# A gated recurrence feeding a feed-forward block: tanh of the input gate written in place, more load buffers, and a new order of the whole program

## The chip, the core and the metric

The kernel runs on one core of a Trainium2 chip. A core has five engines that run their own instruction streams and meet only at semaphores: TensorE (PE in the profile, with its weight loads apart as PEld), VectorE (DVE), ScalarE (ACT), GpSimd (POOL) and SyncE (SP), which here issues all transfers but one. Each engine executes in order: an instruction that waits holds up all behind it. The metric is the time of one execution on the device, in microseconds. The kernel before took 522.07 us, the median of six runs (520.51 to 523.22).

## The reference

Inputs are x, r_gate and i_gate of shape (4, 5824, 256) in float32, a_param (256), and four weight matrices. What is computed, cut to what matters:

```python
sig_r, sig_i = 1 / (1 + exp(-r_gate)), 1 / (1 + exp(-i_gate))
a_t = exp(8.0 * sig_r * log(a_base))          # a_base: sigmoid of a_param, clipped
x_gated = sqrt(max(1 - a_t * a_t, 1e-6)) * sig_i * x
for t in range(S):
    h = a_t[:, t] * h + x_gated[:, t]         # h = 0 at the start of each of 4 sequences
    y[:, t] = h
a = y @ w1; b = y @ w2                        # 256 -> 1024
out = ((a * b) @ w3) @ w_out                  # 1024 -> 1024 -> 256
```

## The kernel before

The 23296 tokens are cut into 47 chunks: two of 256 tokens, 44 of 512, one of 256. A chunk c goes through a chain of steps, each of which is one small function with a one-letter name. The letters are those of the order quoted below; a number after them is the chunk, and further numbers are the half (the 256 channels are two blocks of 128) or the part.

- r, i, x (line 128): SP loads the three inputs, 512 KB each, tokens on the partitions, into the pool `loads`, which has three buffers for each of the three names.
- R and I (lines 137, 139, 146): ACT takes tanh of half of r and of i (a sigmoid is a tanh, scaled and shifted). Tanh of i goes to a tile of its own, th_i, in float32, with two buffers.
- p, t (lines 151, 167, 170): one is added to th_i in place, and it is multiplied by x, which gives u in bfloat16.
- V, U (lines 177, 188): th_r and u are turned, so that channels lie on the partitions: for the chunks in TURN_R and TURN_U by PE with the identity, into PSUM, for all others by a DMA transpose that SP issues, into SBUF.
- d, s, q, g (lines 199 to 224): ACT makes the decay a = exp(...); its square comes from ACT, DVE or POOL; ACT takes the root; DVE multiplies root and u.
- h, y (lines 241 to 250): DVE runs the recurrence as a scan, one for each half; the result is cast to bfloat16.
- a, b (line 260): PE makes eight blocks of 128 columns of y @ w1 (a) and y @ w2 (b). A block of a takes one PSUM buffer, b two blocks at a time.
- c, m (lines 274, 276, 288): ACT or DVE copies a to SBUF, DVE multiplies it with b out of PSUM.
- D, e, o (lines 299, 274 or 276, 318): PE multiplies with the folded matrix w3 @ w_out, ACT or DVE copies the result out, SP stores it.

The fold of w3 and w_out into one matrix is computed at the start in eight pieces: Lw3 loads, Cw3 casts, Ft transposes on PE, Fc copies out, Fm multiplies, Fe copies out with a scale (lines 345 to 407). The first D needs all eight. W steps are groups of eight matmuls of the identity with itself (line 255), with a result that nobody reads. PSUM has two pools: `psum_o` with four buffers, which a, D, the turned tiles and the fold share, and `psum_b` with two, which b and W share. A buffer is taken in the program's order, and is free when the reader of its former tile is done.

Nothing of the order is found at run time. All steps stand in one long text, ORDER, and the program issues them word by word in that order; each engine so gets its own part of the text. The sets ahead of it tell which engine does a step: DV_ names a step given to DVE, AC_, FOLD_ACT and W_ACT to ACT, and POOL has what is left where it can. The order begins so:

```
i1 r1 E A3. A0. A1. A2. r0 I1 R1 i0 R0 V1 V0 W1 W12 I0 x1 d1.0 s1.0 t1.1 W2 x0 U1 d0.0 W0 d0.1 t0.1 d1.1 s0.0
s1.1 Lw1.0 Lw2.0 Cw1.0 r2 Lw1.1 s0.1 q1 g1 U0 i2 q0 Cw2.0 Lw2.1 R2 W15 W4 r3 W3 W8 Lw3.2 g0 h0.0 W7 W6 h0.1
```

Of the kernel before, what the change touches and what calls it, by code (L numbers as in the profile page):

```python
# [10 lines left out]
F32 = mybir.dt.float32  # L11
BF16 = mybir.dt.bfloat16
AF = mybir.ActivationFunctionType
# [9 lines left out]
def kernel(  # L23
# [12 lines left out]
    nc = tc.nc  # L36
    P = 128
    B, S, D = x.shape
# [17 lines left out]
    loads = ctx.enter_context(tc.tile_pool(name="loads", bufs=3))  # L56
    gates = ctx.enter_context(tc.tile_pool(name="gates", bufs=2))
# [20 lines left out]
    T = {}  # L78

    TURN_R = {0, 1, 2, 3, 4, 7, 12}  # L80
    TURN_U = {0, 1, 2, 3, 4, 6, 7}
    DV_TIMES = {0, 1}
    DV_PLUS = set()
    DV_HALF = {(8, 0)}
    DV_SQUARE = {(0, 0), (1, 1)}
    AC_SQUARE = {(3, 1), (4, 1), (5, 0), (5, 1), (7, 0), (8, 1), (9, 0), (11, 0), (11, 1), (12, 0), (12, 1), (13, 0),
        (13, 1), (14, 0), (14, 1), (15, 1)}
    DV_CAST = {1, 2}
    AC_CAST = {0}
# [35 lines left out]
    def load(c, nm):  # L125
        n = sizes[c] // P
        t = loads.tile([P, 4, D], F32, name=nm + "_t", tag=nm)
        nc.sync.dma_start(  # L128
            out=t[:, :n, :],
            in_=src[nm][starts[c]:starts[c] + sizes[c], :].rearrange("(p n) c -> p n c" if long_rows(c) else "(n p) c -> p n c", p=P))  # L130
        T[nm, c] = t
# [11 lines left out]
    def tanh_i(c):  # L143
        n = sizes[c] // P
        t = gates.tile([P, 4, D], F32, name="th_i", tag="th_i")
        nc.scalar.activation(out=t[:, :n, :], in_=T["i", c][:, :n, :], func=AF.Tanh, scale=0.5)  # L146
        T["thi", c] = t
# [261 lines left out]
    def last(c):  # L409
# [21 lines left out]
        i1 r1 E A3. A0. A1. A2. r0 I1 R1 i0 R0 V1 V0 W1 W12 I0 x1 d1.0 s1.0 t1.1 W2 x0 U1 d0.0 W0 d0.1 t0.1 d1.1 s0.0  # L431
        s1.1 Lw1.0 Lw2.0 Cw1.0 r2 Lw1.1 s0.1 q1 g1 U0 i2 q0 Cw2.0 Lw2.1 R2 W15 W4 r3 W3 W8 Lw3.2 g0 h0.0 W7 W6 h0.1
        h1.0 h1.1 x2 V2 W10 y0 a0.0.1 a0.0.0 b0.0 d2.0 y1 d2.1 I2 W9 a0.1.0 c0.0.0 c0.0.1 m0.0 a1.0.1 a1.0.0 a0.1.1
        b0.1 c0.1.0 c0.1.1 m0.1 a1.1.0 s2.0 Cw1.1 c1.0.0 c1.0.1 Cw2.1 Lwo.1 a0.2.0 c0.2.0 R3 b1.0 a1.1.1 m1.0 W13
        a0.3.0 c0.3.0 b1.1 c1.1.0 a0.3.1 a0.2.1 s2.1 c1.1.1 m1.1 Lwo.0 b0.2 p2 Cw3.2 b0.3 Lw3.0 c0.2.1 a1.2.0 Ft2 m0.2
        c0.3.1 m0.3 b1.2 a1.2.1 q2 c1.2.0 Fc2 c1.2.1 m1.2 t2.0 t2.1 Cwo.1 Cwo.0 r4 W11 V3 U2 Lw3.1 a1.3.0 W14 Lw3.4
        d3.0 d3.1 W5 Fm2 Cw3.0 c1.3.0 g2 h2.0 h2.1 i3 i4 a1.3.1 b1.3 Ft0 R4 Fe2 V4 c1.3.1 Lw3.7 y2 Cw3.4 Fc0 a2.0.0
        a2.0.1 b2.0 Cw3.1 d4.0 d4.1 a2.2.0 m1.3 c2.0.0 I3 s3.0 s4.0 s3.1 c2.2.0 c2.0.1 m2.0 Ft4 a2.1.0 s4.1 I4 a2.1.1
        b2.1 Fm0 Fc4 x3 q3 Lw3.5 Fm4 c2.1.0 c2.1.1 m2.1 Ft1 Lw3.6 p3 Fe0 Fe4 Fc1 Cw3.7 Ft7 a2.3.0 a2.2.1 b2.3 t3.0
        Lw3.3 Fc7 r5 a2.3.1 c2.2.1 t3.1 Cw3.5 U3 c2.3.0 r7 c2.3.1 q4 p4 g3 Cw3.6 Fm1 Ft5 Cw3.3 Ft6 b2.2 Fe1 Fc5 h3.0  # L440
        h3.1 y3 Fm7 R5 Fm5 Fe5 x4 Ft3 Fc6 i5 Fm6 Fc3 t4.0 Fe7 r6 a3.1.0 R7 Fe6 a3.1.1 V5 Fm3 m2.2 c3.1.0 c3.1.1 a3.0.0
        V7 I5 d7.0 c3.0.0 m2.3 i6 r9 t4.1 x5 U4 d7.1 Fe3 g4 h4.0 h4.1 R6 r8 V6 x6 r11 a3.0.1 b3.0 p5 y4 I6 d5.0 t5.0
        b3.1 D0.0 D0.1 e0.0 c3.0.1 m3.0 m3.1 R9 D1.0 D1.1 a3.2.0 e1.0 s5.0 d5.1 s7.0 a3.3.0 a3.2.1 b3.2 b3.3 c3.2.0
        t5.1 o0.0 i7 U5 c3.3.0 c3.2.1 d6.0 a4.0.0 a3.3.1 x7 d6.1 p6 s7.1 s5.1 s6.0 s6.1 m3.2 t6.0 a4.1.0 a4.0.1 b4.0
        o1.0 c4.0.0 t6.1 c3.3.1 m3.3 r10 c4.1.0 R8 a4.3.0 D2.0 D2.1 V8 a4.2.0 c4.0.1 c4.3.0 q5 m4.0 c4.2.0 a4.1.1 e2.0
        g5 i8 h5.0 h5.1 q6 q7 c4.1.1 D2.2 a4.3.1 a4.2.1 D2.3 b4.1 D3.0 D3.1 b4.2 e2.1 y5 m4.1 I7 c4.3.1 V9 e3.0 d8.0
        a5.0.0 d8.1 i10 c4.2.1 m4.2 o2.1 x8 o2.0 b4.3 a5.0.1 I8 p7 R10 c5.0.0 c5.0.1 s8.0 t7.0 i9 t7.1 U6 b5.0 a5.2.0
        a5.1.0 m4.3 d9.0 s8.1 g6 o3.0 m5.0 c5.1.0 D4.0 D4.1 s9.0 c5.2.0 R11 b5.1 a5.1.1 p8 e4.0 c5.1.1 h6.0 D3.2 d9.1
        t8.0 h6.1 m5.1 t8.1 D3.3 a5.3.0 U7 g7 e3.1 r12 V10 o4.0 y6 c5.3.0 I9 I10 h7.0 a5.2.1 b5.2 a5.3.1 a6.1.0 c5.3.1
        d10.0 d10.1 c5.2.1 b5.3 D4.2 m5.2 m5.3 D4.3 c6.1.0 h7.1 R12 e4.1 p10 a6.0.0 a6.0.1 s9.1 b6.0 x10 c6.0.0 a6.2.0  # L450
        c6.0.1 r13 a6.2.1 a6.1.1 o3.1 m6.0 c6.2.0 c6.1.1 q9 a6.3.0 b6.1 c6.2.1 b6.2 m6.1 q8 s10.0 a6.3.1 V12 x9 U8 i11
        D5.0 b6.3 m6.2 c6.3.0 c6.3.1 m6.3 V11 p9 t10.0 t10.1 r14 D5.1 U10 y7 s10.1 t9.0 d12.0 a7.1.0 R13 i13 a7.0.0
        d12.1 e5.0 V13 c7.1.0 a7.0.1 x11 r15 b7.0 a7.2.0 b7.1 a7.2.1 t9.1 g8 d11.0 c7.0.0 c7.0.1 h8.0 h8.1 o4.1 I11
        D6.0 a7.1.1 m7.0 d11.1 c7.2.0 c7.1.1 m7.1 I13 D6.1 y8 s11.0 a7.3.0 c7.2.1 c7.3.0 b7.2 a7.3.1 c7.3.1 e6.0 d13.0
        d13.1 a8.0.0 a8.1.1 a8.1.0 D5.2 b7.3 m7.2 D5.3 U9 c8.0.0 x13 R14 c8.1.0 c8.1.1 m7.3 r16 a8.0.1 g9 p11 h9.0
        s11.1 q10 h9.1 c8.0.1 e5.1 q11 D6.2 D6.3 t11.0 t11.1 p13 t13.0 y9 o6.0 o5.0 U11 V14 R15 b8.0 g10 m8.0 e6.1
        D7.0 a8.2.0 D7.1 b8.1 e7.0 c8.2.0 m8.1 a8.3.0 h10.0 a8.3.1 s13.0 s13.1 a9.0.0 t13.1 c8.3.0 d14.0 h10.1 c8.3.1
        a8.2.1 c9.0.0 c8.2.1 b8.2 a9.0.1 b8.3 a9.1.0 i12 x12 i15 r17 o5.1 y10 m8.2 a9.1.1 m8.3 c9.0.1 c9.1.0 D7.2 I12
        D7.3 c9.1.1 b9.0 b9.1 a9.2.0 V15 I15 a9.3.0 d14.1 R16 i16 r19 o6.1 p12 t12.0 t12.1 m9.0 s14.0 e7.1 c9.2.0
        a10.0.0 a9.3.1 c9.3.0 m9.1 d15.0 p15 c10.0.0 g11 h11.0 h11.1 V16 o7.0 D8.0 c9.3.1 s12.0 s14.1 s15.0 D8.1 x15  # L460
        a9.2.1 U13 R19 i14 a10.0.1 U12 e8.0 d16.0 I16 d16.1 b9.2 D8.2 a10.2.0 b9.3 D8.3 c9.2.1 m9.2 m9.3 c10.0.1 y11
        d15.1 a10.2.1 a10.3.0 b10.0 e8.1 c10.2.0 c10.2.1 s15.1 c10.3.0 a10.1.1 a10.1.0 b10.1 a10.3.1 m10.0 R17 s16.0
        a11.0.0 s12.1 t15.0 t15.1 p16 I14 s16.1 b10.2 c10.1.0 c10.1.1 m10.1 m10.2 p14 a11.2.0 b10.3 c10.3.1 a11.0.1
        a11.1.0 r18 o8.0 x14 x16 b11.0 m10.3 t14.0 q12 t14.1 c11.0.0 o7.1 b11.1 g12 h12.0 h12.1 c11.1.0 U15 D10.0 q13
        c11.2.0 q14 D10.1 c11.0.1 y12 V17 D10.2 D10.3 a11.1.1 t16.0 e10.0 e10.1 c11.1.1 a11.2.1 c11.2.1 x18 q15 q16
        m11.0 m11.1 g13 h13.0 o8.1 V19 i18 a11.3.0 a11.3.1 o10.0 c11.3.0 c11.3.1 D9.0 h13.1 y13 b11.2 D9.1 a12.0.0
# [103 lines left out]
    for word in ORDER.split():  # L570
        name, args = re.fullmatch(r"([LC]w[123o]\.|A\d\.|[A-Za-z]+)([\d.]*)", word).groups()
# [29 lines left out]
```

## Time and profile before

| | before |
|---|---|
| median of six runs | 522.07 us (520.51 to 523.22) |
| the profiled execution | 520.51 us |
| its span, first to last instruction | 518.7 us |
| granted TensorE clock | 1.0 |
| DMA queue of SP: bytes, share of 16 engines | 123.5 MB, 85.4% |
| DMA transposes: number, median from issue to landing | 80, 4.7 us (of r) and 4.2 us (of u) |
| loads of 512 KB: median from issue to landing | 5.5 us (r), 5.5 us (i), 5.1 us (x) |
| table loads on ACT | 34, 1.28 us each |

The span is what the profile covers; what lies around it is 1.8 us. Busy times of PE are not PE at its peak: a matmul is in the pipeline longer than it keeps the next from starting, so the time from one start to the next tells more. "Idle before, releaser" in a row is how long the engine stood before that instruction and what ended it.

### The profile page before, as it was taken

The numbers are of one execution on the slowest core, as the hardware profiler recorded it, in microseconds if no ns is written. First come the engines' busy times: TensorE is split into PE (matmuls) and PEld (weight loads), VectorE is DVE, ScalarE is ACT, GpSimd is POOL, SyncE is SP. The second block draws the span as 40 slices with busy tenths as digits, with TensorE's granted clock in tenths as the row PEclk, the third lists the DMA queues.
The fourth block names the chain that finished last, engine by engine and source line by source line (L and its number), as shares of the span: only waits on it lengthen the run. The fifth ranks groups of instructions, "written<-read, shape, count | busy, mean of one in ns | idle before, by whom it ended". The sixth has DMA issues, their size and how long they took to land.

```text
span 518.7 us, 9092 instructions
## 1 busy us (share of the span) xinstructions
PE 499.7 (96%) x3259; PEld 313.7 (60%) x3313; DVE 437.7 (84%) x422; ACT 466.1 (90%) x715; POOL 314.2 (61%) x268
## 2 busy tenths in 40 slices
PE   5879999999999999999999999999999999999997
PEld 5757665556565566556556565565665566566656
DVE  5998999999999798699898779798788976959853
ACT  6988999999999999999999999999999859968443
POOL 2674856665746855966789956868662767361300
PEclk9999999999999999999999999999999999999999
DMA  8995999999999999979699988999799468452212
GB/s 297 411 412 182 278 346 305 255 311 287 309 264 264 259 273 268 260 206 274 181 309 266 266 236 214 254 317 260 202 246 282 131 209 160 108 180 63 61 62 102
DMA packets 178338, 124.09 MB, mean 239 GB/s; under 512 B 87410, under 2 KB 173940, under 8 KB 178292
## 3 DMA queue, kind: packets, MB, share of 16 engines
q1 hardware_dynamic: 178288, 123.50, 85.4%
q8 instruction: 26, 0.43, 0.4%
q14 instruction: 20, 0.16, 0.1%
q10 hardware_dynamic: 4, 0.00, 0.0%
HBM read 78.91 MB, written 23.86 MB: 198 GB/s over the span
## 4 chain that ended last, share of the span: by engine, by line
PE 77%; DVE 15%; issue 4%; ACT 2%; DMA 1%; SPq 0%; DVEq 0%; ACTq 0%
PE po L299 25%; PE pb L260 25%; PE pa L260 24%; DVE g_t L288 5%; DVE h_t L241 4%; DVE sa L274 3%; DVE nrm L224 1%; PE pw L370 1%; DMA x_t<-in_x_dram 1%; DVE nrm L221 1%; PE ptw L359 1%; ACT sa L276 0%; PE ptr L177 0%; SPq L128 0%; DVE u_t L167 0%
## 5 line engine op out<-in xcount | busy, mean ns | idle before, releaser
L288 DVE TENSOR_TENSOR g_t<-sa,pb 128x1024 bf16<-128x1024 bf16 (+1 forms) x188 | 218.6, 1179 | 64.6 <-PE pb L260 35.6
L260 PEld LDWEIGHTS <-w_sb 128*128 128x128 bf16 x1504 | 146.5, 98 | 150.4 <-issue 8.1
L276 ACT CAST sa<-pa 128x512 bf16<-128x512 f32 (+1 forms) x331 | 179.5, 591 | 28.1 <-PE pa L260 20.9
L260 PE MATMUL pa<-y_t,w_sb 128*128 128x512 bf16 (+1 forms) x720 | 187.7, 372 | 4.6 <-DVE w3t L274 2.9
L260 PE MATMUL pb<-y_t,w_sb 128*128 128x512 bf16 (+1 forms) x730 | 182.7, 372 | 3.0 <-DVE g_t L288 1.1
L299 PE MATMUL po<-wp_sb,g_t 128*128 128x256 bf16 x1456 | 176.8, 273 | 0.5 <-DVE g_t L288 0.4
L299 PEld LDWEIGHTS <-g_t 128*128 128x128 bf16 x1456 | 142.3, 98 | 39.7 <-DVE g_t L288 0.7
L250 POOL CAST y_t<-h_t 128x1024 bf16<-128x1024 f32 (+1 forms) x44 | 51.5, 1170 | 144.9 <-DVE h_t L241 132.9
L241 DVE TENSOR_TENSOR_SCAN h_t<-a_t,h_t,nrm 128x512 f32<-128x512 f32 (+1 forms) x92 | 126.4, 1399 | 2.0
L170 POOL TENSOR_TENSOR u_t<-th_i,x_t 128x512 bf16<-128x512 f32 (+1 forms) x89 | 118.0, 1340 | 2.2 <-DMA x_t<-in_x_dram 1.1
L209 POOL TENSOR_TENSOR nrm<-a_t 128x512 f32<-128x512 f32 (+1 forms) x76 | 88.4, 1176 | 13.5 <-ACT a_t L199 13.5
L276 ACT COPY ot<-po 128x512 f32<-128x512 f32 (+1 forms) x87 | 51.1, 590 | 15.7 <-PE po L299 14.2
L199 ACT ACTIVATE a_t<-rt,la 128x512 f32<-128x512 bf16 (+1 forms) x80 | 64.7, 824 | 0.2
L151 POOL TENSOR_SCALAR th_i<-th_i 128x1024 f32<-128x1024 f32 (+1 forms) x45 | 52.2, 1160 | 20.4 <-ACT th_i L146 20.2
L224 DVE SCALAR_TENSOR_TENSOR nrm<-nrm,ut 128x1024 f32<-128x1024 f32 (+1 forms) x40 | 54.0, 1353 | 0.1
L146 ACT ACTIVATE th_i<-i_t 128x1024 f32<-128x1024 f32 (+1 forms) x47 | 49.0, 1047 | 0.5 <-DMA i_t<-in_i_gate_dram 0.4
L213 ACT ACTIVATE nrm<-nrm 128x1024 f32<-128x1024 f32 (+1 forms) x47 | 48.3, 1039 | 0.2
L139 ACT ACTIVATE th_r<-r_t 128x1024 bf16<-128x1024 f32 (+1 forms) x40 | 42.3, 1060 | 0.3 <-DMA r_t<-in_r_gate_dram 0.3
L274 DVE CAST sa<-pa 128x512 bf16<-128x512 f32 (+1 forms) x45 | 26.5, 617 | 1.1 <-PE pa L260 0.4
L213 ACT ACT_TABLE_LOAD x17 | 21.8, 1283 | 1.4 <-DVE nrm L209 1.1
L199 ACT ACT_TABLE_LOAD x9 | 11.5, 1283 | 0.2
L255 PE MATMUL warm<-ident 128*128 128x128 bf16 x128 | 9.9, 238 | 0.3 <-DVE g_t L288 0.3
(58 smaller groups left out, 128.7 us busy)
## 6 DMA issues: line engine op xcount, KB each, us to landing
out_dram<-ot SPq DMA_DIRECT2D x90, 256.0 KB, 3.9
r_t<-in_r_gate_dram SPq DMA_DIRECT2D x44, 512.0 KB, 5.5
i_t<-in_i_gate_dram SPq DMA_DIRECT2D x44, 512.0 KB, 5.5
x_t<-in_x_dram SPq DMA_DIRECT2D x44, 512.0 KB, 5.1
wf<-in_moe_w_dram SPq DMA_DIRECT2D x12, 512.0 KB, 9.6
wf<-in_moe_w_out_dram SPq DMA_DIRECT2D x2, 512.0 KB, 11.1
i_t<-in_i_gate_dram SPq DMA_DIRECT2D x3, 256.0 KB, 4.5
r_t<-in_r_gate_dram SPq DMA_DIRECT2D x3, 256.0 KB, 3.3
```

Source lines behind the costliest of these rows:

```text
L151: (nc.vector if c in DV_PLUS else nc.gpsimd).tensor_scalar(t, t, 1.0, 1.0, op0=ALU.add, op1=ALU.mult)
L170: (nc.vector if (c, half) in DV_HALF else nc.gpsimd).tensor_mul(out=u, in0=t, in1=xt)
L199: nc.scalar.activation(out=a, in_=pr, func=AF.Exp, scale=la4[:, cb:cb + 1], bias=la4[:, cb:cb + 1])
L209: (nc.vector if (c, cb) in DV_SQUARE else nc.gpsimd).tensor_mul(out=n, in0=a, in1=a)
L213: nc.scalar.activation(out=T["n", c][:, :, :w], in_=T["n", c][:, :, :w], func=AF.Sqrt, scale=-1.0, bias=1.0)
L224: nc.vector.scalar_tensor_tensor(out=T["n", c][:, :, :w], in0=T["n", c][:, :, :w], scalar=1e-3, in1=T["pu", c][:, :, :w], op0=ALU.max, op1 ...
L241: nc.vector.tensor_tensor_scan(h[:, cb, :], a[:, cb, :], n[:, cb, :], init, ALU.mult, ALU.add)
L250: eng.tensor_copy(out=T["y", c][:, :, :w], in_=T["h", c][:, :, :w])
L260: nc.tensor.matmul(out=dst[:, :w], lhsT=w_sb[:, cb, m * P:(m + 1) * P], rhs=T["y", c][:, cb, :w], start=(cb == 0), stop=(cb == NCB - 1))
L276: nc.scalar.copy(out=dst, in_=src_ps)
L288: nc.vector.tensor_mul(out=T["g", c][:, 2 * mp:2 * mp + 2, :w], in0=T["sa", c, mp][:, :, :w], in1=T["pb", c, mp][:, :, :w])
L299: nc.tensor.matmul(out=po, lhsT=T["g", c][:, k, j * P:(j + 1) * P], rhs=wp_sb[:, k, :], start=(k == 0), stop=(k == KD - 1), skip_group_che ...
```

## The change

Three things are changed. First, tanh of the input gate is written over the tile that was loaded, so there is no tile th_i any more, and p and t work on the load's tile. Second, the loads get buffers of their own numbers: four for r, five for i, four for x, in place of three each. Third, the order and the sets that tell which engine does a step are replaced as a whole. Chunk 5's u is turned by PE instead of by a DMA. The counts: DVE has 37 copies of a instead of 45, no cast of y instead of two, six evacuations instead of four; ACT has 339 copies of a instead of 331, two casts of weights instead of five, 86 evacuations instead of 88; POOL has 46 casts of y instead of 44 and eleven of weights instead of eight. ACT loads its tables 34 times in both. The order's text differs in nearly every line.

```diff
-    TURN_U = {0, 1, 2, 3, 4, 6, 7}
+    TURN_U = {0, 1, 2, 3, 4, 5, 6, 7}
...
-    DV_HALF = {(8, 0)}
-    DV_SQUARE = {(0, 0), (1, 1)}
+    DV_HALF = {(2, 0)}
+    DV_SQUARE = {(0, 0), (1, 0), (10, 0)}
...
-    DV_CAST = {1, 2}
-    AC_CAST = {0}
+    DV_CAST = set()
+    AC_CAST = {4}
...
-    DV_EVAC = {(2, 1), (5, 0), (9, 0), (9, 1)}
-    FOLD_ACT = {('c', 3), ('c', 6), ('e', 1), ('e', 2), ('e', 6)}
-    W_ACT = {('w2', 1), ('w3', 0), ('w3', 1), ('w3', 2), ('w3', 5)}
-    W_DVE = {('w1', 0)}
+    DV_EVAC = {(1, 0), (2, 0), (3, 1), (5, 1), (9, 0), (9, 1)}
+    FOLD_ACT = {('c', 7), ('e', 0), ('e', 1), ('e', 2), ('e', 3), ('e', 7)}
+    W_ACT = {('w2', 0), ('w3', 6)}
+    W_DVE = {('w1', 1)}
+    LOAD_BUFS = {"r": 4, "i": 5, "x": 4}
...
-        t = loads.tile([P, 4, D], F32, name=nm + "_t", tag=nm)
+        t = loads.tile([P, 4, D], F32, name=nm + "_t", tag=nm, bufs=LOAD_BUFS[nm])
...
-        t = gates.tile([P, 4, D], F32, name="th_i", tag="th_i")
-        nc.scalar.activation(out=t[:, :n, :], in_=T["i", c][:, :n, :], func=AF.Tanh, scale=0.5)
+        t = T["i", c]
+        nc.scalar.activation(out=t[:, :n, :], in_=t[:, :n, :], func=AF.Tanh, scale=0.5)
```

The beginning of the new order, as far as the first matmul of chunk 4 (a4.0.1):

```
r0 r1 E A3. A0. A1. i1 R1 R0 W3 V1 I1 V0 W13 W12 A2. W9 d1.0 d1.1 s1.0 i0 W15 I0 x0 t0.1 W14 d0.0 s0.0 s1.1
d0.1 s0.1 q0 x1 t1.1 Lw1.0 r3 Lw2.0 r2 q1 R3 Lw1.1 i2 W11 U0 g0 h0.0 Lw2.1 Cw1.0 W10 W2 U1 W0 W7 R2 W4 h0.1
Lw3.2 x2 g1 y0 W8 Lwo.0 Cw2.0 a0.1.0 a0.1.1 h1.0 c0.1.0 h1.1 a0.0.0 a0.0.1 V2 c0.1.1 d2.0 c0.0.0 W6 y1 b0.0
c0.0.1 d2.1 I2 Cw1.1 a1.0.1 a1.0.0 b0.1 a1.1.0 a0.2.0 c1.0.0 c1.0.1 Cw2.1 p2 a0.2.1 Cw3.2 m0.0 m0.1 c1.1.0
Lwo.1 b1.0 m1.0 t2.0 r4 W1 c0.2.0 a1.1.1 a0.3.0 t2.1 Cwo.0 W5 c1.1.1 Ft2 c0.2.1 a1.3.0 s2.0 b1.1 c0.3.0 b0.2
U2 a1.3.1 s2.1 Cwo.1 i3 Fc2 V3 x3 Lw3.0 q2 Lw3.1 i4 Lw3.4 m1.1 c1.3.0 Fm2 R4 g2 h2.0 h2.1 d3.0 Lw3.7 c1.3.1
m0.2 d3.1 Lw3.5 Fe2 a1.2.0 a0.3.1 b1.2 a1.2.1 I3 c0.3.1 V4 s3.0 d4.0 d4.1 b0.3 y2 c1.2.0 Cw3.0 c1.2.1 m1.2
a2.0.0 a2.1.0 b1.3 m0.3 a2.2.0 b2.0 m1.3 a2.2.1 c2.0.0 Lw3.3 a2.0.1 s4.0 c2.2.0 s3.1 p3 t3.0 c2.1.0 Cw3.1 Ft0
c2.0.1 c2.2.1 Fc0 m2.0 Cw3.4 b2.1 I4 s4.1 q4 r7 t3.1 a2.3.0 a2.1.1 Fm0 b2.2 p4 Cw3.5 c2.1.1 Ft4 c2.3.0 m2.1
Fe0 Ft1 a2.3.1 U3 Lw3.6 q3 Fc4 c2.3.1 Fc1 Fm4 Cw3.7 b2.3 Ft5 g3 Fe4 Fc5 Ft7 x4 Cw3.3 R7 r5 h3.0 h3.1 Fm1 Fm5
Fc7 Fe5 Ft3 Fm7 Fe1 Cw3.6 V7 Fe7 y3 Ft6 Fc3 d7.0 d7.1 Fc6 m2.2 Fm3 i6 r6 a3.1.0 Fe3 R5 Fm6 a3.1.1 c3.1.0
c3.1.1 t4.0 Fe6 t4.1 i7 i5 x5 U4 a3.0.0 R6 D0.0 a3.0.1 D0.1 I6 c3.0.0 e0.0 m2.3 g4 a3.3.0 a3.2.0 b3.0 h4.0
h4.1 b3.1 c3.0.1 m3.0 D1.0 a3.3.1 D1.1 I5 c3.3.0 y4 V5 r8 m3.1 a3.2.1 V6 b3.2 I7 e1.0 c3.2.0 c3.2.1 c3.3.1
b3.3 m3.2 m3.3 p5 a4.0.1
```

## The prediction

> **What bounds the kernel now.** First the busy shares, then what one matmul costs in the chain of waits (columns: start, length, what), then the engines in stretches of 20 us.
>
> ```profile
> PE 499.7 (96%) x3259; PEld 313.7 (60%) x3313; DVE 437.7 (84%) x422; ACT 466.1 (90%) x715; POOL 314.2 (61%) x268
> ...
> 173.57 1.73 PE pb L260 x8
> 175.73 1.75 PE po L299 x16
> ```
>
> Eight up-projection matmuls of 512 columns start within 1.73 us, 0.216 us each; sixteen of 256 columns within 1.75, 0.109 each. From the program: 44 full chunks x 32 x 0.216 = 304.1; three half chunks x 32 x 0.109 = 10.5; 1456 down-projections x 0.109 = 159; the fold's 64 matmuls 7.0 and 64 transposes 3.6 (0.0555 each); 96 turning transposes 5.3. Together 490 us of PE work that no order removes (128 warm-up matmuls, 7 us, are filler). The span is 518.7: everything to be won is 28.7 us. A rule of the Trainium skill ("Perfetto Trace Analysis", Identifying the Most-Contended Engine) judges PE's headroom by the share of weight loading: 60% here, 205 us free. The matmuls' own starts leave 28.7; I use these.
>
> ```profile
> core 0: us, PE busy (x) PEld busy (x) DVE busy (x) ACT busy (x) POOL busy (x), PEclk, DMA share, GB/s
> 0.00:20.00 20.00, 12.69 (x154) 11.86 (x155) 13.26 (x36) 15.19 (x23) 6.55 (x13) 1.00 0.90 336
> 20.00:40.00 20.00, 16.20 (x173) 12.79 (x172) 19.26 (x30) 18.32 (x24) 16.66 (x15) 1.00 1.04 412
> 40.00:60.00 20.00, 19.84 (x163) 13.98 (x164) 17.77 (x23) 18.66 (x27) 9.97 (x10) 1.00 0.75 197
> 60.00:80.00 20.00, 19.73 (x132) 12.58 (x133) 19.55 (x22) 19.93 (x29) 13.04 (x12) 1.00 1.10 345
> 80.00:100.00 20.00, 19.74 (x123) 11.43 (x124) 19.58 (x21) 19.71 (x29) 13.55 (x11) 1.00 1.04 256
> 100.00:120.00 20.00, 18.95 (x116) 11.25 (x116) 19.76 (x21) 19.67 (x30) 10.44 (x9) 1.00 1.09 306
> ...
> 480.00:500.00 20.00, 19.89 (x124) 12.17 (x125) 15.82 (x15) 10.65 (x20) 4.39 (x6) 1.00 0.21 65
> 500.00:520.00 20.00, 15.67 (x128) 12.33 (x126) 6.75 (x8) 6.68 (x16) 0.24 (x1) 0.98 0.23 79
> ```
>
> 19.89 of 20 is a saturated PE. The loss lies in the first 33 us, in small gaps from 60 to 140 us, and in the last evacuation and store (the last matmul starts at 515.5, 3.2 us to the end). In 60 to 120 DVE and ACT both have 19.6 of 20: two engines limit PE there at once. The first saturated moment is in the order of time, PE alone:
>
> ```profile
> 29.41 0.62 PE L177 MATMUL ptr<-ident,th_r 128*128 128x128 bf16 x8 [0.21 <-ACT th_r L137]
> 32.88 1.02 PE L260 MATMUL pa<-y_t,w_sb 128*128 128x512 bf16 x3 [2.85 <-DVE w3t L274]
> ```
>
> By 32.88 PE has done chunks 0 and 1 (64 x 0.109 = 7.0), 48 turning transposes (2.7) and 1.8 of the fold: 11.4. So 21.5 us are lost before it; 28.7 - 21.5 - 3.2 leaves 4.0 for gaps after it. Those are the three pots.
>
> **The change part by part.**
>
> Buffers and Tanh in place. Tanh keeps its instruction and size (1.076 us, 128x1024); only its target moves. A load tile of the input gate is now held until the product, five buffers for the three plus two of before. In the list of waits the engines stood for loads of r, i and x 3.2 us in all: ACT 0.4 and 1.4 in the first 7 us, POOL 1.1 and ACT 0.3 later, none of it on PE. So earlier loads win 0. SP's side: nothing in the new order blocks it before the transpose V5, so 30 loads follow each other at the head's 412 GB/s; before, SP stood from 34 to 46 us, and the GB/s fell to 182. Earlier loads take nothing that PE waits for, but they fill the queue ahead of transposes, which take 4.7 us to land and 9.1 at worst; the order leaves them as long (7.4 us of PE work in the median between V and its decay, 6.9 before). Taken as 0; bounds -1 and +5 (one decay standing for a landing).
>
> Chunk 5's u turned on PE: 8 x 0.0555 = **+0.44**, on the path since PE is saturated; one DMA transpose less from SP.
>
> DVE to ACT to POOL. DVE loses 8 copies out of PSUM (0.6 each), two casts of y (1.35, 0.43) and one fold piece, and gains two evacuations (0.67) and a square: about -4.6 us. ACT gains 8 copies (0.55), one fold piece and a square, and loses 3 weight casts (1.05) and two evacuations (0.59): +0.6. POOL +2.5, with 39% idle. Table loads stay 34.
>
> The head, walked with durations of the rows. PE, up to its first use: the loads land one per 1.27 us (512 KB at 412 GB/s), so R1 runs at 4.1, I1 at 6.1, d1 at 6.8, I0 at 7.7, d0.1 ends at 9.7; s0.1 on POOL (0.72) ends at 10.5, and from there ACT does not rest. Its list up to the fold's Fe7: six table loads 7.7, roots q0 q1 q2 q4 q3 4.4, R3 R2 R4 R7 4.3, I2 I3 I4 3.2, six decays 4.4, seven half copies 2.6, four whole ones 2.3, five squares 3.2, two weight casts 2.1, Fe2 Fe0 Fe1 Fe7 1.6, Fc7 1.0: 36.8, so 47.3. PE meanwhile: y0 on POOL is ready at 15.2 (before 15.7), but b0.0 waits for the weights w2 cast by ACT at 17.5 (before 16.6). y2 is ready at 30.4: g2 26.8, two scans 2.5, POOL 1.05; before 32.2, because the scans took 3.2 beside POOL's cast and DVE cast y2 itself. So PE gets chunk 2 two us earlier. It can't use it: PSUM slots come free late, as h2 on DVE stands ahead of m0.2, c1.2.0, m1.2, m0.3, m1.3 (32.9), and a2.2.1 waits for the decay d4.1 (ACT 33.7), a2.3.0 for c2.2.0 (35.5), U3 for Fe0 (40.5), V7 for Fe1 (45.9), Ft6 for Cw3.6 (47.0). After Fe7: d7 and Fe3 2.05, R5 1.07, two copies 1.2, R6 I6 2.13, c3.0.0 0.6: 54.3. Then PE: a3.2.0 0.43, b3.0 b3.1 1.73, D1.0 0.88, a3.3.1 0.43, D1.1 0.88, a3.2.1 0.43, b3.2 b3.3 1.73: 60.8, plus some eight hand-overs of 0.07 to 0.1 (R4 ends 29.35, V4 starts 29.41): **61.5** at a4.0.1, with 38.85 us of work behind it (chunks 0 to 3 20.8, fold 10.6, D0 and D1 3.5, 72 turning transposes 4.0). Before reaches 38.85 at 32.88 + 27.45 = 60.3. Head: **+1.2**, bounds -1 (the y2 lead is used) and +3 (each hand-over is missed twice).
>
> The gaps of 60 to 140, about 2.5 of the 4.0. Counted along both orders by the rows' durations, from 40 to 100 us of PE work DVE's share falls from 66.5 to 63.9, ACT's stays (66.3, 66.5). A product needs both halves of its copies, so it is as late as the later engine, and ACT has 0.7 us idle in 60. DVE's relief alone wins 0; if DVE was the only limit it wins 1.9. I take 0: the eight copies land on the engine that is as full.
>
> Rest and tail: both orders end in b46.3, D45.2, D45.3, m46.2, m46.3, D46.0, D46.1; the two D hide the last products (1.75 over 1.4). 0.
>
> The clock. Warm-up matmuls show it (24 in 2.76 us at half speed, 48 in 2.84 at full):
>
> ```profile
> 7.19 2.76 PE L255 MATMUL warm<-ident 128*128 128x128 bf16 x24
> ...
> 11.01 2.84 PE L255 MATMUL warm<-ident 128*128 128x128 bf16 x48
> ```
>
> The new order spends 13 of the 16 warm-up groups by 12.5 us, then PE has nothing until 15.2. "TensorE: Matmul & The Clock Gate" (Part 1: The HAM clock gate) halves the clock after an idle window of about 3.4 us: a gap 0.7 longer than mine would put up to 3.4 us of work at half speed, +1.7. The trace's own gap before 32.88 is 2.85 and the next matmuls run full. I take 0.
>
> Sum against the profiled execution (520.5 us, 1.8 around its span): +0.44 + 1.2 = +1.64, 522.2. The six runs' median 522.07 lies 1.56 above the profiled one; the same addition gives **523.8**.
>
> **The rivals.**
>
> *DVE was the limit* (ends faster). For: products and scans of DVE fill the chain of waits from 75 to 137 us, and copies can be put off on ACT by delaying tanh of later chunks. Then the 60 to 140 gaps go (-2.5), y2's two us are used (-1): 522.07 + 0.44 - 3.5 = 519.0. Against: ACT's 19.9.
>
> *A transpose lands late* (slower). With up to 30 loads queued, decay or product of one chunk stands in ACT's or DVE's order until a landing of 9.1 rather than 4.7: 4.4 us on an engine with no rest, all copies behind it, on top of mine: 528. Against: 0.2 us of such waits now, and 7.4 us of lead. It decides when the lead falls under the landing.
>
> *The change cancels*: ACT's head is 1 us shorter than walked, or half of the DVE relief comes back: 522.5.
>
> **How the numbers follow.** 0.3% is 1.6 us: under 520.5 is faster, over 523.6 slower, about what a measurement here can tell. Forecast 0.47 (own range 522.6 to 526, a quarter of it within 0.3%); faster rival 0.31; late transpose 0.13; cancelled 0.09. So faster 0.31, same 0.12 + 0.09 = 0.21, slower 0.35 + 0.13 = 0.48. The range goes to 518.5, under the DVE rival, and to 529, over the late transpose.
>
> **What would show it.** Right: chunk 4's first matmul at 61 to 62 us; ACT with no idle from 11 to 47; PE busy under 19.9 in 60 to 120 still. Wrong: that matmul at 60 or before; PE at 19.89 from 60 on with DVE below 19; a gap of ACT ended by a landing of rt; matmuls of 128 columns at 0.107 us after 12 us.

## The result and the profile after

The changed kernel takes 519.73 us (median of 21 runs, 517.69 to 520.39), the kernel before, run beside it, 521.93 (42 runs). The ratio is 0.9954, 95% interval 0.9942 to 0.9965: 0.46% faster, where 523.8 was forecast and slower was held the likeliest. The two profiled executions, however, are almost equal: 520.39 after, 520.51 before; spans 518.5 and 518.7.

The page of the changed kernel, busy shares and the granted clock in 40 slices:

```profile
PE 502.4 (97%) x3267; PEld 316.5 (61%) x3321; DVE 425.6 (82%) x414; ACT 466.2 (90%) x720; POOL 315.7 (61%) x271
...
PEclk9979999999999999999999999999999999999999
```

DVE is busy 12.1 us less than before, ACT as long as before. Most of the 12.1 is no work that was moved away: 9.4 are the same 88 scans of 512 columns, which took less time on the mean (rows of before, then of after: busy us, mean ns). In the second profile of the changed kernel, told of below, they are 118.2 us, 1373 ns.

```profile
L241 DVE TENSOR_TENSOR_SCAN h_t<-a_t,h_t,nrm 128x512 f32<-128x512 f32 x88 | 123.5, 1429 | 1.9
L241 DVE TENSOR_TENSOR_SCAN h_t<-a_t,h_t,nrm 128x512 f32<-128x512 f32 x88 | 114.1, 1327 | 1.9
```

The third digit of the clock is a 7. The engines in stretches of 20 us, columns as in the prediction:

```profile
0.00:20.00 20.00, 15.46 (x179) 14.22 (x180) 12.18 (x35) 16.99 (x28) 5.88 (x13) 1.00 0.92 336
20.00:40.00 20.00, 16.26 (x120) 10.88 (x119) 14.53 (x23) 15.61 (x22) 15.11 (x15) 0.83 1.04 412
...
60.00:80.00 20.00, 19.89 (x136) 12.64 (x136) 19.83 (x22) 19.91 (x28) 13.97 (x14) 1.00 1.17 312
...
100.00:120.00 20.00, 18.65 (x117) 11.45 (x118) 18.05 (x19) 19.56 (x29) 11.86 (x10) 1.00 0.95 278
...
500.00:520.00 20.00, 15.47 (x132) 12.67 (x130) 6.84 (x8) 6.64 (x16) 0.00 (x0) 0.98 0.23 80
```

The clock column reads 0.83 from 20 to 40 us, where before had 1.00. PE's busy time there is as long as before, but part of it is matmuls that take twice their time, as the order of time shows (PE alone; start, length, what, idle time before it and what ended that):

```profile
28.48 0.58 PE L260 MATMUL pa<-y_t,w_sb 128*128 128x256 bf16 x2 [3.08 <-DVE sa L274]
28.86 1.06 PE L260 MATMUL pb<-y_t,w_sb 128*128 128x256 bf16 x4
29.72 0.63 PE L260 MATMUL pa<-y_t,w_sb 128*128 128x256 bf16 x2
30.14 1.06 PE L177 MATMUL ptr<-ident,th_r 128*128 128x128 bf16 x8
31.00 1.06 PE L260 MATMUL pb<-y_t,w_sb 128*128 128x256 bf16 x4
31.85 0.63 PE L260 MATMUL pa<-y_t,w_sb 128*128 128x512 bf16 x1
```

The four matmuls at 28.86 are followed 0.86 us later: 0.215 each, where 256 columns cost 0.109. The eight of 128 columns take 0.86 as well, 0.107 each instead of 0.0555. From the end of the stand of 3.08 us to about 34 us everything runs at half the clock. The instruction that stood is a0.3.1; the program gave it the PSUM bank of a1.2.0, just written, so it waits for the copy c1.2.0, and that stands on DVE behind g2, both scans of h2 and m0.2 (it runs from 28.01 to 28.43).

To compare executions, read the start of a matmul from the order of time and take off the PE work that the order puts ahead of it (0.216, 0.109, 0.0555 a matmul; warm-up ones not counted). What remains is the time **lost so far**. A row is the first matmul of the step; after_again is the second profile of the changed kernel:

| lost before (us) | before | after | after_again |
|---|---|---|---|
| a2.0.0, first of chunk 2 | 21.5 | 21.3 | 19.9 |
| a4.0.0 (before), a4.0.1 (after), first of chunk 4 | 21.6 | 22.6 | 19.9 |
| b9.3 | 24.2 | 24.1 | 21.4 |
| b15.3 | 24.9 | 25.2 | 22.6 |
| D46.1 | 26.4 | 25.7 | 23.2 |

Before to after, profile to profile: head +1.0, gaps behind it 4.8 to 3.1 (-1.7), chunk 5's transposes +0.45 of work: -0.2, the difference of the spans (518.7, 518.5). Before to after_again, two executions that both kept the clock: head -1.7, gaps -1.5, transposes +0.45: -2.7, again the difference of the spans (518.7, 516.0).

### The profile page after: what moved, and what is told of

Read it like the earlier page. It is cut to its first block, busy times and chain, and to the rows that moved or that the text cites. A ratio compares the mean times of both kernels' runs of the same rounds, so it can differ in the third digit from the quotient of the medians.

```text
span 518.5 us, 9045 instructions
## 1 busy us (share of the span) xinstructions
PE 502.4 (97%) x3267; PEld 316.5 (61%) x3321; DVE 425.6 (82%) x414; ACT 466.2 (90%) x720; POOL 315.7 (61%) x271
## 4 chain that ended last, share of the span: by engine, by line
PE 85%; DVE 7%; DMA 3%; issue 3%; ACT 2%; SPq 0%; DVEq 0%; ACTq 0%
PE po L299 28%; PE pb L260 27%; PE pa L260 27%; DVE g_t L288 2%; DMA x_t<-in_x_dram 2%; DVE h_t L241 2%; PE pw L370 1%; DVE nrm L224 1%; DMA wf<-in_moe_w_dram 1%; PE ptr L177 1%; DVE sa L274 1%; PE ptw L359 1%; SPq L128 0%; ACT sa L276 0%; ACT L213 0%
## 5 line engine op out<-in xcount | busy, mean ns | idle before, releaser
L276 ACT CAST sa<-pa 128x512 bf16<-128x512 f32 (+1 forms) x339 | 182.6, 588 | 29.8 <-PE pa L260 23.2
L170 POOL TENSOR_TENSOR u_t<-i_t,x_t 128x512 bf16<-128x512 f32 (+1 forms) x89 | 123.7, 1407 | 6.0 <-issue 3.3
L241 DVE TENSOR_TENSOR_SCAN h_t<-a_t,h_t,nrm 128x512 f32<-128x512 f32 (+1 forms) x92 | 117.0, 1302 | 1.9
L209 POOL TENSOR_TENSOR nrm<-a_t 128x512 f32<-128x512 f32 (+1 forms) x74 | 82.7, 1136 | 13.6 <-ACT a_t L199 13.5
L151 POOL TENSOR_SCALAR i_t<-i_t 128x1024 f32<-128x1024 f32 (+1 forms) x45 | 51.0, 1134 | 19.8 <-ACT i_t L146 19.8
L276 ACT COPY ot<-po 128x512 f32<-128x512 f32 (+1 forms) x85 | 49.7, 591 | 13.1 <-PE po L299 12.3
L146 ACT ACTIVATE i_t<-i_t 128x1024 f32<-128x1024 f32 (+1 forms) x47 | 48.9, 1043 | 0.6 <-DMA i_t<-in_i_gate_dram 0.5
L274 DVE CAST sa<-pa 128x512 bf16<-128x512 f32 (+1 forms) x37 | 21.9, 617 | 3.0 <-PE pa L260 2.9
L199 ACT ACTIVATE a_t<-ptr,la 128x512 f32<-128x512 bf16 (+1 forms) x14 | 9.6, 713 | 1.4 <-POOL nrm L209 1.3
```

The lines of the kernel that those rows point to most:

```text
L151: (nc.vector if c in DV_PLUS else nc.gpsimd).tensor_scalar(t, t, 1.0, 1.0, op0=ALU.add, op1=ALU.mult)
L170: (nc.vector if (c, half) in DV_HALF else nc.gpsimd).tensor_mul(out=u, in0=t, in1=xt)
L199: nc.scalar.activation(out=a, in_=pr, func=AF.Exp, scale=la4[:, cb:cb + 1], bias=la4[:, cb:cb + 1])
L209: (nc.vector if (c, cb) in DV_SQUARE else nc.gpsimd).tensor_mul(out=n, in0=a, in1=a)
L241: nc.vector.tensor_tensor_scan(h[:, cb, :], a[:, cb, :], n[:, cb, :], init, ALU.mult, ALU.add)
L276: nc.scalar.copy(out=dst, in_=src_ps)
```

## The experiments

The ones on top of the changed kernel mostly start from clock_fill, whose own runs differ by 0.3 us only. "Kept" means a granted clock of 0.999 or 1.0 over the execution.

**The same kernel twice.** after_again is the changed kernel, unaltered.

> The changed kernel as it is, beside the next run on the same chip. If the result stands: 519.7 within 0.5, most executions with a granted clock of 0.993 to 0.997, those at 0.999 or 1.0 about 1.5 to 2 below the others.

Measured: 519.41 (six runs, 0.9944 of before, 0.9924 to 0.9965). Its profiled execution happened to keep the clock, span 516.0:

```profile
28.62 0.38 PE L260 MATMUL pa<-y_t,w_sb 128*128 128x256 bf16 x2 [3.07 <-DVE sa L274]
28.84 0.60 PE L260 MATMUL pb<-y_t,w_sb 128*128 128x256 bf16 x4
29.27 0.38 PE L260 MATMUL pa<-y_t,w_sb 128*128 128x256 bf16 x2
29.49 0.61 PE L177 MATMUL ptr<-ident,th_r 128*128 128x128 bf16 x8
29.94 0.60 PE L260 MATMUL pb<-y_t,w_sb 128*128 128x256 bf16 x4
30.38 1.03 PE L260 MATMUL pa<-y_t,w_sb 128*128 128x512 bf16 x3
```

The same stand, 3.07 us, and behind it the four matmuls are followed after 0.43 us, not 0.86. Chunk 4 begins at 58.70 instead of 61.39. Over both batches 28 executions of the changed kernel are known: 4 kept the clock (median 517.87), 24 did not (519.78). The clock so costs 1.9 us in the middle. The execution profiled first lost 2.7 by chunk 4; it is one of four that read 0.993 (median 520.38), while the other twenty read 0.996 or 0.997 (519.74).

**The stand filled, or shortened.** clock_fill puts 40 idle matmuls into it, clock_order moves two DVE instructions and adds nothing, before_fill fills the stand of before.

```diff
-    WARM = [8, 8, 8, 8, 8, 8, 8, 8, 8, 8, 8, 8, 8, 8, 8, 8]            (both fills)
+    WARM = [8, 8, 8, 8, 8, 8, 8, 8, 8, 8, 8, 8, 8, 8, 8, 8, 40]
-    a1.2.0 a0.3.1            (clock_fill)
+    a1.2.0 W16 a0.3.1
-    Fm2 R4 g2 h2.0 h2.1 d3.0 Lw3.7 c1.3.1 m0.2 ... a1.2.0 a0.3.1 ... y2 c1.2.0      (clock_order)
+    Fm2 a1.2.0 R4 g2 h2.0 m0.2 c1.2.0 h2.1 d3.0 Lw3.7 c1.3.1 ... a0.3.1 ... y2
-    y2 Cw3.4 Fc0 a2.0.0      (before_fill)
+    y2 Cw3.4 Fc0 W16 a2.0.0
```

> The changed kernel with 40 matmuls of the identity (2.2 us at the 0.0555 us of the warming ones) between a1.2.0 and a0.3.1, where TensorE stands for 3.1 us waiting for c1.2.0. My theory: this stand drops the granted clock to half for some 5 us in most executions, which costs 1.5 to 2.5 us of the kernel; with it filled, the clock reads 1.0 in the records, matmuls from 28.5 on start 0.11 (256 columns) apart, the first matmul of chunk 4 comes at about 59.5 instead of 61.4, and the median falls from 519.7 to about 517.9, which is where the two executions of the changed kernel with a granted clock of 0.999 and 1.0 lie (517.7, 518.2). Rival: the matmuls behind the stand wait for data of other engines anyway (y2 on POOL, the copies on ACT), and a faster clock only moves the wait: the same 519.7 within 0.3.

> The changed kernel with two DVE instructions moved and nothing added: m0.2 and c1.2.0 (whose end frees the PSUM bank of a0.3.1) stand behind h2.0 instead of behind h2.1. Clock theory: c1.2.0 ends at about 27.0 instead of 28.4, TensorE stands 1.7 us instead of 3.1, the clock stays at 1.0; y2 comes some 1 us later (29.5), which the matmuls a0.3.1 to b0.3 (1.8 us at full clock) mostly hide. Median about 517.5 to 518.2. Rival (clock without weight, or y2 the next to be late): 519.5 to 520.5.

> The kernel before with the same 40 matmuls of the identity ahead of a2.0.0, where TensorE stands for 2.9 us from 29.9 to 32.9. In the profiled execution of before this stand did not drop the clock, but that was one of its two or three fastest executions (520.5 against a median of 521.9). Theory: in most of the others it does drop, so the median falls by 1 to 1.5, to about 520.5 to 520.9, and the two kernels differ by about 2.5 still when both keep their clock. Rival: before keeps its clock in all executions and its spread has another cause: 521.9, no change within 0.4.

Measured: clock_fill 517.54 (0.9916, 0.9888 to 0.9945), all six executions at 1.0; clock_order 517.47 (0.9915, 0.9888 to 0.9942), five of six kept, the one at 0.996 took 518.29. The order of time of clock_fill, PE:

```profile
25.41 2.40 PE L255 MATMUL warm<-ident 128*128 128x128 bf16 x40
28.64 0.38 PE L260 MATMUL pa<-y_t,w_sb 128*128 128x256 bf16 x2 [0.84 <-DVE sa L274]
```

a0.3.1 starts no earlier than in the profile of after (28.64 against 28.48), yet chunk 4 begins at 58.72 rather than 61.39. Only idle matmuls were added, so the rival, that the matmuls wait for other engines anyway, falls. In clock_order the bank comes free earlier, and PE then waits 0.38 us for y2 (PE again):

```profile
27.23 0.38 PE L260 MATMUL pa<-y_t,w_sb 128*128 128x256 bf16 x2 [1.91 <-DVE sa L274]
...
29.53 1.02 PE L260 MATMUL pa<-y_t,w_sb 128*128 128x512 bf16 x3 [0.38 <-POOL y_t L250]
```

before_fill: 521.52 against 522.10 beside it (0.9984, 0.9964 to 1.0004), not told apart from no change. But the clocks are: 12 of its 14 executions kept theirs, and of 96 of before that ran beside the experiments only 17 did (median 520.55; the other 79 522.33). So before loses its clock too, and one profile shows where: before_bufs, which comes next and has the order of before, reads 0.997 in it. Behind the same stand its four matmuls of 512 columns take 1.71 us to the next row instead of 0.86 (PE):

```profile
33.43 0.52 PE L261 MATMUL pa<-y_t,w_sb 128*128 128x512 bf16 x1 [2.86 <-DVE w3t L275]
...
35.02 1.91 PE L261 MATMUL pb<-y_t,w_sb 128*128 128x512 bf16 x4
36.73 0.71 PE L261 MATMUL pa<-y_t,w_sb 128*128 128x512 bf16 x2
```

Filling the stand brings back 0.6 of those 1.8. Why not the rest stays open: the 12 executions of before_fill that kept their clock have a median of 521.35, 0.8 above the 17 of before. Where the other two lost theirs is likely an earlier stand, of 1.74 us in the profile of before_fill. Two later kernels with the same start, bfill_act6 and bfill_newsets, lost their clock in 5 of 12 and 5 of 6 executions. In their profiles that stand is 2.16 and 2.32 us long, and half speed follows it (PE of bfill_act6; the four at 16.46 take 0.85):

```profile
15.01 0.62 PE L177 MATMUL ptr<-ident,th_r 128*128 128x128 bf16 x8 [2.16 <-ACT th_r L137]
...
16.46 1.06 PE L260 MATMUL pb<-y_t,w_sb 128*128 128x256 bf16 x4
17.31 1.06 PE L255 MATMUL warm<-ident 128*128 128x128 bf16 x8
```

**The buffers alone, and the order without them.**

```diff
-        t = loads.tile(..., tag=nm)                          (before_bufs: the change's own lines, old ORDER)
+        t = loads.tile(..., tag=nm, bufs=LOAD_BUFS[nm])
...                                                      (before_bufs: LOAD_BUFS and tanh of i in place, as in the change)
-    LOAD_BUFS = {"r": 4, "i": 5, "x": 4}                     (fill_r3x3, on clock_fill)
+    LOAD_BUFS = {"r": 3, "i": 5, "x": 3}
```

> The kernel before, its order and assignments untouched, with the one part of the change that gives it its name: Tanh of the input gate written over its load, and 4, 5 and 4 buffers for the loads. Transfers can start earlier, no engine has less to do. Since only 3.2 us of waits for loads stand in the trace of before and none is ahead of TensorE after 20 us, I expect no gain: 521.9 within 0.4. Rival (the spread of before, 519.6 to 525.1, comes from loads that land late behind three buffers): the median falls by 1 or more and the spread shrinks to that of the changed kernel, some 2.5 us. A third case: loads started earlier meet the writes of outputs and the transposes on the queues and cost up to 3.

> clock_fill (517.5) with three buffers instead of four for the loads of the recurrence gate and of x; the input gate keeps its five. My theory that the added buffers by themselves carry none of the gain: 517.5 within 0.3, the loads that start later still land before they are read. Rival, buffers carry part of it: reads of a load then show waits for DMA in 40 to 140 us and the time rises by 0.5 to 2.

Measured: before_bufs 522.77 against 522.10 (1.0011, 0.9991 to 1.0030), no gain. fill_r3x3 540.71, 3.6% slower than before and 23 us behind clock_fill: far outside both expectations. The waits of SP's queue from 100 to 500 us in fill_r3x3 (who waits for whom: us in all, times, longest):

```profile
SPq L128 <- ACT th_r L139: 29.8, 5, 15.1
...
SPq L128 <- POOL u_t L170: 21.7, 5, 10.5
```

Its order of time, first SP:

```profile
307.79 0.46 SPq L318 DMA_DIRECT2D out_dram<-ot  x1
323.44 0.37 SPq L128 DMA_DIRECT2D r_t<-in_r_gate_dram  x1
...
325.01 1.92 SPq L188 DMA_TRANSPOSE ut<-u_t  x1
```

then DVE, which needs that transpose,

```profile
331.03 1.23 DVE L224 SCALAR_TENSOR_TENSOR nrm<-nrm,ut 128x1024 f32<-128x1024 f32 x1 [11.44 <-DMA ut<-u_t]
```

and PE:

```profile
335.98 1.86 PE L260 MATMUL pb<-y_t,w_sb 128*128 128x512 bf16 x4 [9.90 <-DVE g_t L288]
```

The second row of SP is a load of r that stands so early in the order that with three buffers it waits for the tanh that reads the oldest of them. SP stands 15.1 us in it, with it the stores and transposes behind, and PE loses 9.9 us at the end of the chain. Part of the 23 us is the clock, which such stands take down: the profiled execution was granted 0.984 over 538.7 us, by which up to 8.6 us (an estimate: 0.016 of the span) were lost to half speed. In clock_fill one single load waits for a buffer after 100 us, 2.9 us for a product of POOL. Which of the two buffers matters more, and whether the fifth of the input gate is needed, was not tried.

**Chunk 5's u on the transposing DMA again.**

```diff
-    TURN_U = {0, 1, 2, 3, 4, 5, 6, 7}
+    TURN_U = {0, 1, 2, 3, 4, 6, 7}
```

> clock_fill (517.5) with u of chunk 5 turned by the transposing DMA, as before the change, in the place of TensorE's 8 transposes. By the sum of the prediction TensorE then has 0.44 us less to do: 517.1, if u5 has landed when DVE comes to nrm of chunk 5 (some 3 us behind the issue). Rival, the transposes were put on TensorE because the landing is late in the new order: DVE waits for it in front of h5, chunk 5's y comes later, and the time is 518 to 520.

Measured: 519.02, 1.5 more than clock_fill, as the rival had it. It is seen in the order of time of DVE:

```profile
65.21 1.21 DVE L288 TENSOR_TENSOR g_t<-sa,pb 128x1024 bf16<-128x1024 bf16 x1
68.10 1.23 DVE L224 SCALAR_TENSOR_TENSOR nrm<-nrm,ut 128x1024 f32<-128x1024 f32 x1 [1.68 <-DMA ut<-u_t]
```

DVE stands 1.68 us for the landing, y5 is 1.65 later, and PE waits 1.51 us for it at 72.98.

**Copies between DVE and ACT: both ways in the changed kernel, from DVE to ACT in the kernel before.**

```diff
+    DV_COPY |= {(3, 3, 0), (4, 3, 0), (5, 0, 0), (6, 1, 1), (8, 1, 1), (9, 3, 0)}   (fill_dve6, on clock_fill)
+    DV_COPY -= {(4, 1, 0), (5, 1, 1), (6, 2, 1), (7, 0, 0)}                         (fill_act4, on clock_fill)
+    DV_COPY -= {(3, 3, 0), (4, 3, 0), (5, 0, 0), (6, 1, 1), (8, 1, 1), (9, 3, 0)}   (bfill_act6, on before_fill)
```

> clock_fill (517.5) with six copies of chunks 3 to 9 given back from ACT to DVE (3.3.0, 4.3.0, 5.0.0, 6.1.1, 8.1.1, 9.3.0; 0.68 us of DVE each, 4.1 us in all, against 0.59 of ACT each). Theory of the prediction (DVE and ACT are both full from 60 to 140 us, so what one gains the other loses): 517.5 within 0.5. Rival, DVE was the limit of the kernel before in these stages and its relief is the gain: 519 to 521, with the gaps of TensorE in 60 to 140 us up by 1.5 or more.

> clock_fill (517.5) with the four copies that the change gave to DVE in chunks 4 to 7 (4.1.0, 5.1.1, 6.2.1, 7.0.0) given to ACT: 2.7 us less for DVE, 2.4 more for ACT. If DVE is still the limit after the change: 515.5 to 517. If the change has moved the work to the point where the two are level: ACT is now late instead and the time rises by 1 to 3, to 518.5 to 520.5.

> The kernel before with its stand filled (before_fill, 521.5) and the same six copies taken from DVE to ACT: the mirror image of fill_dve6, which cost 4.3. In 60 to 120 us before has 19.63 of 20 us busy on DVE and 19.77 on ACT. If DVE is the limit and ACT the next with slack in its waits: 519.0 to 520.0, gaps of TensorE in 60 to 140 us down by 1.5 or more. If both are at their limit there (my recorded view): 521.5 within 0.5, the gaps now ended by ACT's copies. If ACT is the tighter one: 523 to 525.

Measured: fill_dve6 521.80 (+4.3 on clock_fill), fill_act4 519.73 (+2.2), bfill_act6 522.47 (+0.95 on before_fill, 1.0007 of before, 0.9993 to 1.0021). The stretch of 60 to 80 us, columns as above, in fill_dve6,

```profile
60.00:80.00 20.00, 19.45 (x131) 12.17 (x132) 19.76 (x22) 18.83 (x25) 13.64 (x13) 1.00 1.06 312
```

in fill_act4

```profile
60.00:80.00 20.00, 19.81 (x137) 12.62 (x137) 18.17 (x19) 19.94 (x29) 13.48 (x14) 1.00 1.02 312
```

and in bfill_act6:

```profile
60.00:80.00 20.00, 18.96 (x124) 11.84 (x125) 18.22 (x19) 19.94 (x29) 13.91 (x13) 1.00 1.09 345
```

With more on DVE it is DVE that stays at 19.76 and ACT that drops; with less, ACT stays at 19.94 and DVE drops; PE loses either way. In clock_fill itself both are full, 19.69 and 19.94. So in the changed kernel the two engines are level, and four to six copies either way are too many; fill_dve6 alone, which cost more than either of its expectations, would have fitted a limit on DVE only.

bfill_act6 does not settle the same for the kernel before. PE's stands of 0.87 and 0.36 us in 77 to 95 us end with copies of ACT, but the two behind them end with DVE: 0.75 us at 99.41 and the longest, 1.56 us, at 118.48 (DVE, POOL and PE of bfill_act6):

```profile
110.71 2.31 DVE L224 SCALAR_TENSOR_TENSOR nrm<-nrm,ut 128x1024 f32<-128x1024 f32 x1
110.67 1.27 POOL L170 TENSOR_TENSOR u_t<-th_i,x_t 128x512 bf16<-128x512 f32 x1 [1.90 <-DMA x_t<-in_x_dram]
118.48 1.24 PE L260 MATMUL pa<-y_t,w_sb 128*128 128x512 bf16 x5 [1.56 <-DVE sa L274]
```

The product of chunk 9 at 110.71 took 1.22 us in before_fill, where POOL was idle; here it ran beside a product of POOL. The edit so brought about a collision, and what the six copies alone would have done stays open. Its five executions without the clock are not the reason: the seven that kept it have a median of 522.31, 1.0 above the twelve of before_fill.

**The old split in the new order, and the reverse.** All assignments of chunks 3 and up are exchanged, ORDER is not.

```diff
-    DV_HALF, DV_SQUARE, AC_SQUARE, DV_CAST, AC_CAST, DV_COPY, DV_EVAC: entries of chunks 3 and up
+    the other kernel's entries of chunks 3 and up
```

> clock_fill (517.5) with the assignment to engines of the kernel before for all work of chunks 3 and up (copies, squares, casts, evacuations); the order stays the new one. If the split carries the smaller gaps: about 519.5. If the order carries them: 517.5 to 518. If each fits only the other (what fill_dve6 and fill_act4 suggest): 520 to 523, worse than either.

> before_fill (521.5) with the new assignment for chunks 3 and up in the old order. If the split carries the smaller gaps: about 519.6. If the order carries them: 521.5 within 0.5. If each fits only the other: 522.5 to 525.

Measured: fill_oldsets 522.45 (+4.9 on clock_fill), bfill_newsets 527.03 (+5.5 on before_fill, more than even its third case). Five of the six executions of bfill_newsets lost the clock, but the one that kept it took 526.01, and in its profile the loss between chunk 4 and b9.3 is 7.3 us, where before_fill has 2.7. So the third case holds: each split fits only its own order. Neither carries the smaller gaps alone.

**Going further.** The largest gap that clock_fill has left behind the head is 1.25 us at 99.6: PE waits for the copy c7.1.1, which stands behind the square s10.0 and m7.0 on DVE. order_fill is clock_order with 24 idle matmuls in what is left of the stand; best_pool adds s10.0 on POOL and m7.0 behind c7.1.1; best_chase adds I13 behind c8.0.1.

```diff
-    h2.0 m0.2 c1.2.0 h2.1 ... a0.3.1                         (order_fill, on clock_order)
+    h2.0 m0.2 c1.2.0 h2.1 ... W16 a0.3.1      with 24 as W16's number in WARM
-    DV_SQUARE = {(0, 0), (1, 0), (10, 0)}                    (best_pool, on order_fill)
+    DV_SQUARE = {(0, 0), (1, 0)}
-    D6.1 m7.0 a7.2.0 D5.0 a7.1.1 ... c7.1.1
+    D6.1 a7.2.0 D5.0 a7.1.1 ... c7.1.1 m7.0
-    R15 I13 a8.0.0 c8.0.0 b7.3 c8.0.1                        (best_chase, on best_pool)
+    R15 a8.0.0 c8.0.0 b7.3 c8.0.1 I13
```

> clock_order with 24 identity matmuls (1.3 us) in what is left of the stand, and nothing of best_pool's later edits. Clock theory: every execution keeps 1.0, the one at 0.996 that clock_order had is gone, median 517.0 to 517.5, 2.2 or more below the changed kernel run beside it. Rival: the difference to clock_order is in the later stages (its 1.25 us wait at 98.8 stays), so 517.5 as before, and no more than 1.5 below the changed kernel.

> The two DVE moves of clock_order, 24 identity matmuls (1.3 us) in the rest of TensorE's stand, and one later edit: the square s10.0, which stands on DVE between h8.1 and m7.0 (0.67 us at 97.2 in clock_fill), goes to POOL, which is idle there from 93.1 to 97.3, and the copy c7.1.1 goes ahead of the product m7.0, so that the bank that TensorE waits 1.25 us for at 99.6 comes free 1.3 us earlier. If TensorE's starts are all that counts: clock_order's 515.2 of span with the clock at 1.0, less 1.2, so 516.0 to 516.5 as the median. If what is late moves to the next wait within 10 us (m7.0, then b7.1): 517.0 to 517.4.

> best_pool (517.75, span 515.5 in its profile) with one instruction moved on ACT: I13 (Tanh, 1.06 us) goes behind the copies c8.0.0 and c8.0.1, for whose bank TensorE waited 1.11 us at 103.7 in best_pool. If that wait was the one that ate the gain of best_pool: 516.3 to 516.9. If ACT as a whole is the limit of this stage, the wait moves on once more: 517.3 to 518.

Measured: order_fill **516.97** (six runs, 516.89 to 518.07; 0.9909 of before, 0.9890 to 0.9928), every execution kept the clock, 2.4 below after_again on the same chip (519.41). best_pool 517.75, best_chase 518.37: the later edits gain nothing. In best_pool the gap at 99.6 is gone and another has come, ended by the other engine (PE, order of time):

```profile
103.69 0.49 PE L299 MATMUL po<-wp_sb,g_t 128*128 128x256 bf16 x3 [1.11 <-ACT sa L276]
```

and on DVE the square's 0.67 us are mostly gone again: the instruction beside which POOL now works (the square, from 92.35 to 93.39) takes 1.74 us, where it took 1.22 in clock_order (DVE of best_pool):

```profile
92.74 1.74 DVE L224 SCALAR_TENSOR_TENSOR nrm<-nrm,ut 128x1024 f32<-128x1024 f32 x1
```

best_chase cuts that wait to 0.17 us, and one of 0.96 us appears at 110.6, ended by DVE. In a stage where two engines are full, taking one stand away moves it on.

## Why the prediction was wrong, step by step

**"The same addition gives 523.8"** is the larger error. The median of before lies 1.56 above its profiled execution; I carried that over as if it lay around any program. It is the clock: the profiled execution of before kept it, as only 17 of 96 do, and the median one did not. After is the other way round, profiled without the clock, its median 0.66 below. That is 2.2 of the 4.1 us by which 523.8 missed.

**"The gaps of 60 to 140: I take 0", "Rest and tail 0"** is the other: behind the first matmul of chunk 4 the loss fell from 4.8 to 3.1 us. (The terms of PE's work add to 489.5 rather than 490, and the gaps were 4.8 rather than 4.0 to begin with.) Up to b15.3 it went from 3.3 to 2.7. The remaining 1.0 lay behind b15.3 in before, for the most part in single stands of 0.54 us at 414.6 and 0.39 at 347.0, of which nothing is left.

What the step leaned on held in the changed kernel: DVE and ACT are level (fill_dve6, fill_act4); for the kernel before that is not shown (bfill_act6). What did not follow is that the gaps stay. The exchange of splits shows that only the pair of order and split has small ones; busy sums cannot tell that. What exactly makes them small is not shown. One candidate was never counted: DVE's term of -4.6 took its instructions as having one length each, and its busy time fell by 12.1 (by 7.7 in after_again). A scan or a product of DVE can take longer while POOL multiplies beside it, and the two late stands of before stand behind such rows (before; DVE, POOL, PE):

```profile
408.74 2.33 DVE L241 TENSOR_TENSOR_SCAN h_t<-a_t,h_t,nrm 128x512 f32<-128x512 f32 x1
409.94 1.96 POOL L209 TENSOR_TENSOR nrm<-a_t 128x512 f32<-128x512 f32 x1
415.15 0.39 PE L299 MATMUL po<-wp_sb,g_t 128*128 128x256 bf16 x2 [0.38 <-DVE g_t L288]
```

Two scans together take 2.46 us where POOL is idle (at 97.5 in the changed kernel). No run changes such a collision alone. The rival "DVE was the limit" came nearest with its 519.0. In the changed kernel ACT limits as much (fill_act4), so its reason does not hold there; for the kernel before the runs do not exclude it.

**Head +1.2**: measured +1.0, and a4.0.1 at 61.39 where 61.5 was walked. The number was right and two of its steps were not. The walk is 2 us late by y2 (30.4; it was done at 28.43): ACT's table load for the first root ran beside s0.1 (8.88 to 10.16) rather than behind it, the cast of w2 was done at 15.67, and b0.0 started at 15.72, not 17.5. "It can't use it" is refuted by after_again, where the lead brings a4.0.1 to 58.70, 1.7 less lost than before. What ate it is **"The clock: I take 0"**, whose bound of +1.7 was set at a stand from 12.5 to 15.2 that PE hardly had, while the one that I had walked (banks late behind h2 on DVE) was priced as waiting only. The half speed cost 1.9 in the median and 2.7 in this profile. So the test "chunk 4's first matmul at 61 to 62" came true for a wrong reason, and only the tests beside it say so: ACT was not free of idle time from 11 to 47 (15.61 of 20 busy in 20 to 40), and matmuls of 128 columns at 0.107 us, listed as a sign against me, were there.

**U5 +0.44**: right as PE work. Its worth was left out: without it DVE stands 1.68 us in the new order.

**Buffers 0**: right for the buffers added alone (before_bufs), wrong as a part of this order, which cannot do without them (fill_r3x3). The rival "a transpose lands late" was thereby real, one step away: it is what the buffers and U5 prevent.

## What to carry to other kernels

Before adding a change to a median, look at whether the profiled execution is like the median one: here the granted clock of each run split both kernels' runs into groups 1.8 to 1.9 us apart, nearly as much as the whole effect of 2.2. Price a stand of the matmul engine of 2 to 3 us twice, for the wait and for the half-speed stretch behind it; idle matmuls or two moved instructions took 2.2 to 2.4 us off. When order, split and buffers come out of one search, testing parts one by one shows only that none carries the gain; ask which stand is next, not which engine is less busy. Before calling a part harmless in one kernel, note what else it moves: an edit of six copies brought a product of DVE and one of POOL together.

## What the runs showed of the hardware

Half speed behind a stand of the matmul engine came in some executions and not in others. The changed kernel kept the clock with 3.07 us in one profile and lost it with 3.08 in the other; it lost it in 24 of 28 executions. The order of before has 2.85 us in one profile (kept) and 2.86 in another (before_bufs, lost), and lost the clock in 79 of 96. Stands of 2.16 and 2.32 us lost it in two profiles, and there the first 16 matmuls behind the stand, from 15.01 to 15.92 in bfill_act6, still ran at full speed. The same place with 1.36 and 1.74 us (before, before_fill) kept it. Filled to 0.84 us, none of six executions lost it; cut to 1.9, one of six. The rule cited in the prediction ("TensorE: Matmul & The Clock Gate", Part 1: The HAM clock gate) speaks of a whole idle window of about 3.4 us; the stands here are shorter and suffice most of the time, so a stand has to be taken as a chance, not as a threshold.

An operation on POOL was not free for DVE: the product of two SBUF tiles went from 1.22 to 1.74 us beside a square (best_pool) and to 2.31 beside a product (bfill_act6), and one scan took 2.33 us where two take 2.46 with POOL idle.
